# A tuned attention and two-layer kernel on one core: front reordered, W1 scaled between its loads, pair 1 in seven products, batch 1 mixed by VectorE

## The chip, the cores and the metric

One core of a Trainium2 chip runs the kernel. The metric is the time of one execution on the device in microseconds (us), given as the median of three runs. Engines: PE multiplies matrices (TensorE, with PEld its weight loads), DVE is VectorE, ACT is ScalarE, POOL is GpSimd, SP is SyncE. POOL and SP issue the transfers (DMAs); every one that converts from float32 to float16 goes through POOL's queue.

## What is computed

The inputs are q, k, v (4 batches, 8 heads, 768 tokens, 64 columns), 8 memory rows per head, a gain vector and two weight matrices W1 (512 x 2048) and W2 (2048 x 512).

```python
for c in range(24):                       # chunks of 32 queries
    keys = concat(mem_k, k[16 before .. 8 after the chunk])   # 8 + 56 rows
    a = softmax(q_c @ keys.T / 8)
    out[c] = a @ concat(mem_v, the same rows of v)
x = out, heads side by side               # (4, 768, 512)
xn = (x - mean) / sqrt(var + 1e-6) * g
y = x + relu(xn @ W1) @ W2
```

## The kernel before, in words

The tokens of a batch are 6 tiles of 128, in all 24 tiles t; two tiles make a pair u, 12 pairs. For each tile the chain is: `qk` (scores on PE, then `below_max` on DVE, a maximum at L325 and a subtraction at L326, then `weights`, the exponential on ACT at L332), `pt` (transpose of the weights on PE, L342, copy on ACT), `val` (`val_products` on PE at L356 into the two-bank tile `two`; `tokens` on DVE, L365 to L372, which divides by the sums and takes the mean; `shift`, which subtracts the mean, on ACT at L383 or POOL at L379), `turn_x` (transpose on PE at L408, DVE copy into xT at L414) and `root` (sum of squares on ACT, inverse square root on POOL). A pair then goes through `up` (8 steps of 8 products at L446 and a relu, L437 on ACT) and down to the output. `up_half` (L458) is `up` for one tile of pair 0.

The down product has two forms. `down` (L467) is the plain one: 8 steps of 4 products with 512 columns (L471), of which the last of each tile adds to the token and stores (L478). `down7` (L538) makes a pair's 2 x 2 blocks with seven products in place of eight: 7 steps of 8 products with 256 columns (L522), each followed by an addition on DVE (L529). It needs four sums of the relu's output (`r_sum`, L516) and four of W2 (`w2_sum`, L501), all on DVE.

Keys and values reach PE as transposes. For batch 0, `turn_k`, `turn_q` and `turn_v` (L214) transpose the raw data, and copies on DVE ("V") or ACT ("A") put it into the streams: `to_stream` (L227), `to_rows` (L234). V of batch 0 is turned back by `v_turn` (L284, copy L295). From batch 1 on, k and q are first interleaved by `mix` (L245, two copies of 96 x 1024 elements), then turned by `later_k` and `later_q` (L254); V is loaded in place by `load_v_head`.

Every engine takes its instructions in the order of the program, written out by hand: a front for pairs 0 and 1 (L597 to L805), and a plan (L807 to L892) that puts each function of pairs 2 to 11 on one of 16 steps of a pair; the even steps end with an `up`, the odd ones with a down step. `banks` and `use` say which PSUM banks the next functions take in turn. `warm` (L590) issues products of zeros that keep PE busy. POOL's loads share eight semaphores in turn, so that the ninth load waits for the first to land. `scale_w1` (L419) multiplies a quarter of W1 by the gain, four pieces a quarter, at L428 on POOL.

## Time and profile before

| what | us |
|---|---|
| median of three runs | 232.29 (232.07 to 232.44) |
| the profiled execution's own time | 232.79 |
| its span from first to last instruction | 231.1 |
| PE's first real stretch without large gaps begins (first `up`, L446) | 31.44 |
| PE's last product starts | 227.0 |

In the timeline a line gives start, duration, engine, source line, operation, the tile written and those read, the count, and in brackets the idle time ahead of it and what ended that. A product's duration includes its latency, so consecutive ones overlap; the spacing of their starts tells how fast PE runs. In the table of stretches, each engine has its busy time in that stretch.

| stretch, us | PE busy | DVE busy | ACT busy | POOL busy |
|---|---|---|---|---|
| 0 to 10 | 8.69 | 4.17 | 2.14 | 8.60 |
| 10 to 20 | 9.51 | 6.68 | 4.87 | 4.96 |
| 20 to 30 | 8.90 | 6.45 | 4.88 | 9.79 |
| 30 to 40 | 8.36 | 5.59 | 6.63 | 9.24 |
| 40 to 50 | 10.00 | 5.21 | 8.88 | 8.51 |
| 50 to 60 | 9.60 | 7.78 | 9.56 | 9.82 |
| 60 to 70 | 10.00 | 5.35 | 6.72 | 4.99 |
| 70 to 80 | 10.00 | 8.98 | 4.71 | 6.39 |
| 80 to 90 | 9.69 | 9.44 | 6.15 | 7.87 |

### The profile page before, as it was taken

Reading aid. Unit: us, or ns where it says so; the run is one execution under the profiler, and the core shown is the slowest. Engines: PE = TensorE matmul, PEld = TensorE weight load, DVE = VectorE, ACT = ScalarE, POOL = GpSimd, SP = SyncE. Lnnn points to the kernel's source line nnn. Section 1 sums busy time; section 2 is a strip of 40 time slices with the busy share of each in tenths; the row PEclk is TensorE's granted clock in tenths of the full one; section 3 lists DMA queues with packets and bytes.
Section 4 is the critical chain, followed back from the end, with each engine's and each line's share of the span. In section 5 each row is a group of like instructions: output and inputs, shape, how many; then the busy total and the mean of one; then the engine's idle time right before and its main releaser. Section 6 shows DMA issues by size and latency. Waiting matters only on the chain.

```text
span 231.1 us, 8487 instructions
## 1 busy us (share of the span) xinstructions
PE 221.9 (96%) x3693; PEld 189.3 (82%) x3693; DVE 156.4 (68%) x365; ACT 128.7 (56%) x241; POOL 114.7 (50%) x197
## 2 busy tenths in 40 slices
PE   7998888999999999999999999999999999999993
PEld 3575776875676889989989999999999999899982
DVE  3476755478288897797577796895684875646372
ACT  2244585999852739739646458468447265344310
POOL 7829998989935694912724945613031121220000
PEclk9999999999999999999999999999999999999999
DMA  5999999999995699873881992943102002011022
GB/s 76 191 206 205 213 215 196 143 114 70 84 179 114 90 120 112 131 99 41 139 119 29 137 156 55 110 89 70 48 0 94 3 3 91 3 45 48 0 94 94
DMA packets 43282, 23.25 MB, mean 101 GB/s; under 512 B 29884, under 2 KB 39676, under 8 KB 43172
## 3 DMA queue, kind: packets, MB, share of 16 engines
q0 software_dynamic: 38320, 14.48, 55.1%
q1 hardware_dynamic: 4924, 8.22, 12.8%
q8 instruction: 29, 0.48, 0.8%
q14 instruction: 9, 0.07, 0.1%
HBM read 29.02 MB, written 6.29 MB: 153 GB/s over the span
## 4 chain that ended last, share of the span: by engine, by line
PE 76%; DMA 6%; ACT 5%; DVE 4%; POOL 4%; issue 2%; POOLq 0%; DVEq 0%
PE upb L446 31%; PE dnb L522 25%; PE dnb L471 5%; DMA w1c<-in_moe_w_ch_dram 4%; PE one L254 3%; PE two L356 3%; PE one L315 3%; PE one L408 2%; DMA V<-in_v_dram 2%; ACT rT L437 2%; PE one L342 2%; POOL raw L111 2%; POOL w1c L428 1%; DVE KT L227 1%; ACT sq L394 1%
## 5 line engine op out<-in xcount | busy, mean ns | idle before, releaser
L446 PE MATMUL upb<-xT,w1c 128*128 128x256 f16 x736 | 94.8, 273 | 0.4 <-DVE xT L414 0.2
L446 PEld LDWEIGHTS <-w1c 128*128 128x128 f16 x736 | 77.9, 114 | 3.2 <-DVE xT L414 0.4
L437 ACT ACTIVATE rT<-upb 128x512 f16<-128x512 f32 x92 | 53.3, 594 | 34.9 <-PE upb L446 32.8
L529 DVE SCALAR_TENSOR_TENSOR xs<-dnb,rstd,xs 128x256 f32<-128x256 f32 x70 | 33.7, 481 | 27.2 <-PE dnb L522 26.7
L332 ACT ACTIVATE P<-sub 128x512 f16<-128x512 f32 x24 | 15.2, 634 | 37.9 <-DVE sub L326 37.9
L522 PEld LDWEIGHTS <-RS 128*128 128x128 f16 x320 | 30.9, 98 | 3.3 <-issue 0.2
L379 POOL TENSOR_SCALAR xn<-xs,nmean 128x512 f16<-128x512 f32 x18 | 13.6, 756 | 37.4 <-PE upb L446 20.6
L522 PE MATMUL dnb<-T,RS 128*128 128x256 f16 x240 | 30.8, 273 | 0.0
L398 POOL TENSOR_SCALAR veps<-ssq 128x1 f32<-128x1 f32 x24 | 4.8, 200 | 44.2 <-ACT sq L394 43.9
L522 PEld LDWEIGHTS <-rT 128*128 128x128 f16 x240 | 22.9, 98 | 2.3
L120 POOL DMA_DIRECT2D V<-in_v_dram x24 | 20.4, 852 | 0.7 <-PE dnb L522 0.7
L522 PE MATMUL dnb<-w2c,rT 128*128 128x256 f16 x160 | 20.6, 273 | 0.0
L516 DVE TENSOR_TENSOR RS<-rT 128x1024 f16<-128x1024 f16 (+2 forms) x21 | 13.9, 661 | 8.9 <-ACT rT L437 8.9
L325 DVE TENSOR_REDUCE nmx<-one 128x8 f32<-128x512 f32 x22 | 15.1, 685 | 4.7 <-PE one L315 4.7
L394 ACT ACTIVATE sq<-xs,nmean 128x512 f16<-128x512 f32 x24 | 17.3, 721 | 0.1
L366 DVE CUSTOM_DVE_ANT_1 xs<-two,rec 128x512 f32<-128x512 f32 x24 | 16.6, 691 | 0.8
L471 PE MATMUL dnb<-w2c,rT 128*128 128x512 f16 x64 | 16.3, 379 | 0.0
L125 POOL DMA_DIRECT2D V<-in_v_dram x24 | 15.9, 662 | 0.0
L326 DVE TENSOR_TENSOR sub<-one,nmx 128x512 f32<-128x512 f32 x22 | 15.2, 692 | 0.8
L347 ACT COPY PT<-one 128x512 f16<-128x512 f16 x21 | 12.2, 587 | 4.1 <-PE one L342 4.0
L402 POOL TENSOR_TENSOR rstd<-veps,mhalf 128x1 f32<-128x1 f32 x24 | 13.4, 560 | 2.0
L227 DVE COPY KT<-one 128x192 f16<-128x192 f16 (+1 forms) x22 | 11.2, 550 | 2.1 <-PE one L214 1.4
(112 smaller groups left out, 320.5 us busy)
## 6 DMA issues: line engine op xcount, KB each, us to landing
out_dram<-xs SPq DMA_DIRECT2D x23, 256.0 KB, 2.4
raw<-in_k_dram POOLq DMA_DIRECT2D x16, 192.0 KB, 5.3
raw<-in_q_dram POOLq DMA_DIRECT2D x12, 192.0 KB, 6.3
w1c<-in_moe_w_ch_dram POOLq DMA_DIRECT2D x4, 512.0 KB, 10.5
w2c<-in_moe_w_ch_dram POOLq DMA_DIRECT2D x4, 512.0 KB, 8.7
V<-in_v_dram POOLq DMA_DIRECT2D x24, 77.0 KB, 4.0
V<-V SPq DMA_DIRECT2D x3, 360.0 KB
V<-in_v_dram POOLq DMA_DIRECT2D x24, 44.0 KB, 3.7
```

The lines of the kernel that those rows point to most:

```text
L120: nc.gpsimd.dma_start(out=V[b % 2][72:128, 0 : NG - 1, h, 0:64], in_=dram(v, base + 16 * D, [[64, 56], [64 * 64, NG - 1], [1, 64]]),)
L125: nc.gpsimd.dma_start(out=V[b % 2][0:32, 1:NG, h, 0:64], in_=dram(v, base + 48 * D, [[64, 32], [64 * 64, NG - 1], [1, 64]]),)
L325: nc.vector.tensor_reduce(out=m, in_=scores, axis=AX.X, op=ALU.max)
L326: nc.vector.tensor_tensor(out=s.rearrange("p (c k) -> p c k", c=8), in0=scores, in1=free(m, 0, [[1, 8], [0, 64]]), op=ALU.subtract,)
L332: nc.scalar.activation(out=P[t % 3], in_=sub[t % 2], func=ACTF.Exp, scale=0.125)
L366: nc.vector.tensor_tensor_reduce(out=x.rearrange("p (h d) -> p h d", h=H), in0=free(two, 0, [[128, 8], [1, 64]]), in1=free(r, 0, [[1, 8], ...
L394: nc.scalar.activation(out=sq, in_=xs[t % 9], func=ACTF.Square, bias=nmean[t % 6], scale=1.0, accum_out=ssq[i],)
L437: nc.scalar.activation(out=o, in_=i, func=ACTF.Relu)
L446: nc.tensor.matmul(out=p[:, 256 * hb : 256 * hb + 256], lhsT=free(w1c[hc // 4][:, dt, :], hc % 4, [[4, 128]]), rhs=xT[u % 3][:, dt, :], st ...
L471: nc.tensor.matmul(out=p, lhsT=rT[u % 2][:, hc, 128 * i : 128 * i + 128], rhs=w2c[hc // 4][:, hc % 4, :], start=(hc == 0), stop=(hc == 15),)
L522: nc.tensor.matmul(out=p[:, 0:256], lhsT=left[:, n, :], rhs=right(n), start=(n == 0 and not add), stop=(n == 7), skip_group_check=add,)
L529: nc.vector.scalar_tensor_tensor(out=x, in0=p[:, 0:256], scalar=rstd[t % 9], in1=x, op0=ALU.mult, op1=ALU.add,)
```

## The change

- In the front, warm products go to the second half of `two` and there are 24 of them in place of 29; the banks are given out differently.
- The first q copies are split: each engine copies the columns of the first score tile, then those of the second.
- `below_max` of tile 1 is taken apart: its maximum comes after the last V^T copy, its subtraction after the first two `v_turn`, both of which DVE now copies, ahead of the first `pt`.
- POOL scales W1's first quarter ahead of the load of the third, and the second ahead of the load of the fourth.
- `mix` of batch 1 is done by DVE throughout and, for its first half, issued earlier, between the ups of pair 1.
- Pair 1's down product becomes `down7` with its sums; W2's last two sums move to steps 2 and 7 of pair 2; in pair 2 `root` moves by a step, the mix of batch 2's first half from step 14 to 10; the last `pt` of batch 1 moves from step 3 to 5 of pair 3.

```diff
-    def to_rows(b, pv, jj, engine, n, oct0):
+    def to_rows(b, pv, jj, engine, n, oct0, lo=0, hi=None):
+        hi = n if hi is None else hi
         copy_on(engine)(
-            out=free(QD[b % 2], 2 * jj * S + 8 * oct0, [[S, 2], [8, n], [1, 8]]),
-            in_=free(pv, 0, [[1, 2], [2, n], [2 * n, 8]]),
+            out=free(QD[b % 2], 2 * jj * S + 8 * (oct0 + lo), [[S, 2], [8, hi - lo], [1, 8]]),
+            in_=free(pv, 2 * lo, [[1, 2], [2, hi - lo], [2 * n, 8]]),
         )
...
-    def qk_products(t):
+    def qk_products(t, p=None):
-        p = slot()
+        p = slot() if p is None else p
...
+    def row_max(t, scores):
+        nc.vector.tensor_reduce(out=nmx[t % 2], in_=scores, axis=AX.X, op=ALU.max)
+    def less_max(t, scores):
+        nc.vector.tensor_tensor(
+            out=sub[t % 2].rearrange("p (c k) -> p c k", c=8), in0=scores,
+            in1=free(nmx[t % 2], 0, [[1, 8], [0, 64]]), op=ALU.subtract,
+        )
...
     load_octets(2, 1, v, 0, 48, 48)
-    load_w1(2)
-    load_w1(3)
...
-    banks["list"] = one + dnb + [upb[0]]
-    warm(7)
+    for c in range(2):
+        for dt in range(4):
+            scale_w1(c, dt, "P")
+        load_w1(2 + c)
+    idle = two[:, 512:1024]
+    warm(7, idle)
+    use(one[0], one[1], dnb[0], dnb[1])
...
-    warm(4)
+    warm(4, idle)
     for j in range(2):
         turn_k(0, 0, j, "VA"[j])
-    warm(1)
-    for j in range(2):
-        turn_q(0, 0, j, "VA"[j])
-    warm(2)
-    s0 = qk_products(0)
-    s1 = qk_products(1)
+    warm(1, idle)
+    q0 = [turn(raw[1][0], j, 32, one[j]) for j in range(2)]
+    for lo in (0, 16):
+        for j in range(2):
+            to_rows(0, q0[j], j, "VA"[j], 32, 0, lo, lo + 16)
+    s0 = qk_products(0, two[:, 0:512])
+    s1 = qk_products(1, dnb[0])
     below_max(0, s0)
+    use(upb[0], upb[1])
     turn_v(0, 0, "A")
     weights(0)
     turn_v(0, 1, "V")
-    warm(4)
+    row_max(1, s1)
+    warm(2, idle)
+    use(dnb[1], one[0], upb[0], upb[1])
+    v_turn(0, "V")
+    v_turn(1, "V")
+    less_max(1, s1)
+    use(one[1])
     pt(0)
-    v_turn(0, "A")
-    banks["turn"] += 1
-    v_turn(1, "V")
-    below_max(1, s1)
+    use(upb[0], upb[1])
     v2 = v_products(2)
     v3 = v_products(3)
     weights(1)
-    warm(1)
+    warm(1, idle)
     val_products(0)
     tokens(0)
     shift(0, "A")
-    warm(4)
+    warm(3, one[1])
+    use(dnb[1])
     pt(1)
-    for c in range(2):
-        for dt in range(4):
-            scale_w1(c, dt, "P")
     v_copy(2, v2, "V")
     v_copy(3, v3, "V")
-    warm(4)
-    banks["list"] = one
+    warm(4, one[1])
+    use(one[0])
     turn_x(0)
...
     up(1, 4)
+    mix(0, 0, "V")
     v_turn(11, "A")
...
     up(1, 6)
+    mix(1, 0, "V")
     root(3)
...
-    mix(0, 0, "V")
-    mix(1, 0, "A")
     down(0, 0)
...
-    mix(1, 1, "A")
+    mix(1, 1, "V")
...
-            at(u, 12, root, a)
+            at(u, 13, root, a)
...
-            at(3, 3, pt, c + 2)
+            at(3, 5, pt, c + 2)
...
-            at(w, 14 if w == 2 else 12, mix, 0, half, "V")
+            at(w, 10 if w == 2 else 12, mix, 0, half, "V")
...
-    at(2, 7, w2_sum, 2)
-    at(2, 9, w2_sum, 3)
-    for u in range(2, NP - 1):
+    at(2, 2, w2_sum, 2)
+    at(2, 7, w2_sum, 3)
+    for u in range(1, NP - 1):
         for m, step in ((0, 0), (1, 1), (2, 3), (3, 5)):
             plan.setdefault((u + 1, step), []).insert(0, (r_sum, (u, m)))
...
-            elif u == 2:
-                down(1, step // 2)
             elif step < 15:
                 down7(u - 1, step // 2)
```

More of the change, by code (lines that the diff above doesn't have):

```diff
@@ L321, in qk_products @@
         return p.rearrange("p (c k) -> p c k", c=8)
-    def below_max(t, scores):
-        m, s = nmx[t % 2], sub[t % 2]
-        nc.vector.tensor_reduce(out=m, in_=scores, axis=AX.X, op=ALU.max)
-        nc.vector.tensor_tensor(
-            out=s.rearrange("p (c k) -> p c k", c=8), in0=scores,
-            in1=free(m, 0, [[1, 8], [0, 64]]), op=ALU.subtract,
-        )
+    def row_max(t, scores):
[5 more added lines that the diff above has]
+        )
+    def below_max(t, scores):
+        row_max(t, scores)
+        less_max(t, scores)
     def weights(t):
```

## The prediction

> **What bounds the kernel now.** I read the page's first two parts, then stretches, then the timeline wherever TensorE (PE) waits.

> ```profile
> PE 221.9 (96%) x3693; PEld 189.3 (82%) x3693; DVE 156.4 (68%) x365; ACT 128.7 (56%) x241; POOL 114.7 (50%) x197
> ...
> PE   7998888999999999999999999999999999999993
> ```

> PE looks full throughout, but a busy PE need not be at its peak. The spacing of its starts tells more: 256-column products follow each other at 109 ns when nothing holds them. Summed over stretches, starts later than that spacing cost 4 to 5 us in each ten up to 40 us, and about 1 us in each ten after that, mostly the 0.1 us that each change of kind takes. So two things move the end: PE work removed after 40 us, and when the front (0 to 31 us, a chain of small steps) hands over to dense work.

> The front in the timeline (start, duration, engine, line, tile; idle time and releaser in brackets):

> ```profile
> 10.19 1.04 PE L593 MATMUL upb<-zeros 128*128 128x512 f16 x2
> 10.30 0.58 ACT L234 COPY QD<-one 128x512 f16<-128x512 f16 x1 [0.67 <-PE one L214]
> 11.15 1.04 PE L315 MATMUL dnb<-KT,QD 64*32 64x64 f16 x64
> ...
> 16.66 0.69 DVE L326 TENSOR_TENSOR sub<-dnb,nmx 128x512 f32<-128x512 f32 x1
> 17.27 0.20 DVE L365 RECIPROCAL rec<-two 128x8 f32<-128x8 f32 x1
> ...
> 18.08 5.36 POOL L428 TENSOR_SCALAR w1c<-w1c,g_col 128x512 f16<-128x512 f16 x8
> ...
> 18.43 0.72 ACT L383 ACTIVATE xn<-xs,nmean 128x512 f16<-128x512 f32 x1 [0.41 <-DVE nmean L372]
> ...
> 20.83 0.92 PE L458 MATMUL upb<-xT,w1c 128*128 128x128 f16 x13 [0.38 <-POOL w1c L428]
> 21.68 0.53 PE L214 MATMUL one<-identity,raw 96*64 96x96 f16 x16
> ```

> The scores wait for two warm products; the token normalisation waits for DVE's second subtraction; the first up products wait for POOL's W1 scaling. Later:

> ```profile
> 50.54 1.98 ACT L245 COPY raw<-raw 96x1024 f16<-96x1024 f16 x2
> 50.72 0.51 PE L254 MATMUL upb<-identity,raw 96*128 96x96 f16 x8 [0.23 <-DVE raw L245]
> ...
> 53.93 0.50 PE L254 MATMUL upb<-identity,raw 96*128 96x96 f16 x8 [0.18 <-ACT KT L227]
> ```

> ```profile
> 81.34 0.38 PE L342 MATMUL one<-identity,P 128*128 128x128 f16 x4 [0.31 <-DVE KT L227]
> ```

> These three starts come 0.41, 0.34 and 0.47 us after the normal spacing.

> **Part 1, the front.** I walk the chain with the durations above.

> Query copies. One of 512 columns takes 0.70 us on DVE and 0.58 on ACT; of 1024, 1.23 and 1.01. By that slope 256 columns take 0.43 and 0.37 (estimate; bounds zero and the whole 512-column row). ACT's first half starts at 10.30, ends 10.67; the two warm products are gone, so scores start at 10.7 for 11.15: 0.45 earlier.

> First half of the scores (0.64 us to its last result): the maximum starts at 11.4, subtraction ends 12.8, DVE's V^T copies run 13.2 to 14.2, the second maximum ends at 14.8, two V copies (0.42 each, overlapping) at 15.6, the second subtraction at 16.2. It ended at 17.35, so DVE's queue is 1.1 ahead. On PE the V turns now stand ahead of the transpose of the first weights: it moves from 14.54 to 14.6, ACT's copy to 15.6. The values then start at 15.7 for 16.26, and the reciprocal at 16.2 for 17.27, since the second subtraction no longer ends after them. ACT does the second exponential at 16.25 to 16.9, the shift at 17.3 for 18.43: **1.1 earlier**. Turn of x at 18.1, xT done at 19.0.

> W1. Landings (semaphores): first two quarters at 12.8 and 16.2. Eight scalings of 0.67 us (5.36/8) end their halves at 15.5 and 18.9, before xT. So the up products start at 19.0, run in one piece (0.9 us), and the k turn starts at 20.0 for 21.68. The second shift ends at 20.9 (22.05 before); its turn starts at 21.0 for 22.58, and the second half's q turn at 21.95 for 23.66 as it waits for DVE's copy. **Gain 1.7 us**, which the rest inherits.

> What W1 pushes back: loads of quarters 3 and 4 go out at 15.6 and 19.0 instead of 13.1 and 16.5. Ahead of them in the one POOL queue are transfers that land until 22.6, so it never runs empty, and landings stay at about 25.2 and 27.7. The w2 issues behind them come at about 20 and 23, earlier than 23.39 and 26.48. Quarters 3 and 4 are scaled by 27.9 and 30.6 (33.0 before); their users need them at 29.7 and 33.4. If that cover were gone, each us of a late landing past 29.7 would cost one. Batch 1's k and q still land at 38.7 to 50.7 in queue order, and are first used at about 42 and 46, with the pairs behind at about 51 and 55.

> Two gaps called "issue" stay: 0.66 at 26.79 and 0.94 at 38.59. They lie 512 PE instructions apart and the page counts 29 instruction packets of 0.48 MB: PE waits for its own code. The instruction stream keeps its length within some ten, so I cost them at nothing; bounds from both gone (-1.6) to half again as long (+0.8).

> **Part 2, batch 1's interleave.** DVE's mixes (0.75 a pair) go to 44.2 and 48.1, where DVE idles 2.18 us (before 46.38) and 1.18 us (before 49.31). ACT loses 1.98 us at 50.54 and 2.00 at 58.83. The k turn at 50.72 then waits for nothing (0.41). The token chain, DVE idle, starts at 50.5 for 50.92, the shift ends at 52.2 for 53.14, the first k copy at 53.0 for 53.88, while PE would reach the q turn at 53.2: the 0.34 goes too. **0.75 us.** If the mixes met a busy DVE instead, they'd cost up to 0.75 each; raw data landed long before.

> **Part 3, pair 1 by seven products.** Eight quarter products (0.86 to 0.87 us) become seven of 0.87: PE loses **0.8 us**. DVE gains four sums (0.68 each) and seven additions (0.48) for two of 0.75: +4.6 us. In the stage from 59.6 to 77.7 the stretches show DVE 12.4 of 18.1 us busy. The added work fills that: sums and the first w2 difference fit into the 3.8 us in which DVE waits for scores (before 64.43), but the first maximum comes some 0.3 us late, so the second exponential delays the relu behind it by about 0.25 and the fifth up product with it. By my queue of DVE (each at its spacing) it catches up by the end of pair 2; PE arrives at pair 3 some 0.8 to 1.0 earlier. There the weights' transpose at step 5 no longer meets the k copy (0.47 gone), but the second k turn then waits about 0.55 for the subtraction that frees its bank. Net **0.6 to 0.7**. Bounds: 1.3 (both stalls free) and, if half of the 5.7 us idle can't be used, -1.0.

> **Sum.** 1.7 + 0.75 + 0.65 = 3.1 us. Against the profiled execution's 232.79 that gives 229.7; the three plain runs have a median of 232.29, 0.5 lower, so I forecast **229.2 us** for them.

> **A rule on the clock.** Warm products follow each other at 0.43 us until 13.55 and at 0.216 from about 14.0 on, though the granted clock reads 1.00 in every stretch. Five of 29 go. [...] The trace agrees with half rate up to 13.55; what decides it no row shows.

> **Rivals.**
> - *The forecast*, all three parts: 228.4 to 230.0. Chance 0.62.
> - *DVE binds pairs 2 and 3.* Part 3 then returns nothing or loses up to 1.0, parts 1 and 2 stay: 229.8 to 230.9. For: no idle DVE from 60.6 to about 76 in my queue, and 15.0 of 18.0 us busy in the next stage. Against: the idle lies ahead of the point where it is needed. Chance 0.15.
> - *The front gives back its gain*: the doubling a look later, or the two code waits growing by what is saved between them (they end 2.3 us after their packets start): parts 2 and 3 plus 0.5, 230.4 to 231.4. Chance 0.11.
> - *Slower: the clock stays halved until the dense work.* Place: 14 to 31 us. PE's starts there need about 5.8 us per ten at full rate, so 9.9 us; twice that, with the 7.1 us of gaps absorbing only about half, costs 5 to 6 us against a gain of 3.1: 234 to 235. It decides once half rate lasts past about 24 us (5.8 us of added issue, half of it on the path). For: warm products removed. Against: ten to fourteen us of the same transposes remain. Chance 0.08.
> - *No effect*: the landings, not the chain, set the front. Against: every landing precedes its use by over 1 us. 232.3. Chance 0.04.

> **Range.** 228.2 to 231.0: the forecast's span, DVE's rival, and part of the third. A measurement of this kernel can tell about 0.2% from no change, 0.46 us: faster 0.88, same 0.04, slower 0.08.

> **What would show it.** Right: scores' products at 10.7, shift at 17.3, first up products in one piece near 19.0, k turn near 20.0, dense up products at 29.7 for 31.44; no stall at the first batch-1 turn; no four-quarter products after pair 0; 0.6 us or more between the shift of the starts at 58 us and at 90. Wrong: 0.43 us warm spacing after 14; an up product waiting for w1c; PE waits on DVE longer than 0.3 us between 58 and 85; code waits that grow.

## The result and the profile after

The changed kernel takes 233.63 us (median of six runs, 233.03 to 234.04) beside 232.39 for the kernel before (six runs, 232.07 to 232.70): ratio 1.005, 95% interval 1.0033 to 1.0067. It is **slower by 0.5%**, where 229.2 was forecast and 231.0 was the upper end of the range. The profiled execution took 233.83, its span is 232.1.

Lines of the changed kernel (numbers shifted by the new functions): up L452, relu L443, seven-product down L528 with additions L535 and sums L522, maximum L325, subtraction L328, exponential L338, weights' transpose L348, values L362, tokens L371 to L378, shift L389 (ACT) or L385 (POOL), x transpose L414, mix L246, batch 1's and later turns L255, k turn L214, scaling of W1 L434, warm products L599.

The page of after, its first two parts (busy time of each engine, then 40 slices of 5.8 us):

```profile
PE 218.9 (94%) x3712; PEld 190.6 (82%) x3712; DVE 162.8 (70%) x380; ACT 124.6 (54%) x237; POOL 115.6 (50%) x197
...
PE   7699987999998799999999999999999999999993
```

PE's busy time fell by 3.0 us, but the span grew by 1.0, so PE now waits 4 us more. Behind the first 41 us one place in the row of digits shows it, the 87 at slices 13 and 14 (70 to 81 us), where the page of before had 99. The table of stretches says the same. First after, then before (stretch, then busy time and count of PE, PEld, DVE, ACT, POOL, the granted clock, DMA):

```profile
70.00:80.00 10.00, 7.81 (x164) 6.69 (x162) 6.74 (x17) 3.50 (x8) 4.00 (x8) 1.00 0.65 122
```

```profile
70.00:80.00 10.00, 10.00 (x173) 7.47 (x172) 8.98 (x21) 4.71 (x11) 6.39 (x10) 1.00 0.53 90
```

All engines are less busy than before in that stretch, so none of them is the bound; something that is not an engine holds them. The timeline of after there, one line from each link:

```profile
65.33 1.17 POOL L111 DMA_DIRECT2D raw<-in_k_dram  x2
...
70.62 0.42 PE L362 MATMUL two<-V,PT 64*32 64x65 f16 x32
...
73.22 0.76 DVE L246 COPY raw<-raw 96x1024 f16<-96x1024 f16 x2 [2.80 <-DMA raw<-in_k_dram]
73.90 0.20 DVE L371 RECIPROCAL rec<-two 128x8 f32<-128x8 f32 x1
75.19 0.69 POOL L385 TENSOR_SCALAR xn<-xs,nmean 128x512 f16<-128x512 f32 x1 [3.25 <-DVE nmean L378]
...
75.94 0.40 PE L414 MATMUL one<-identity,xn 128*128 128x128 f16 x4 [1.48 <-POOL xn L385]
...
77.10 0.63 ACT L338 ACTIVATE P<-sub 128x512 f16<-128x512 f32 x1 [5.78 <-DVE sub L328]
...
78.27 1.03 PE L452 MATMUL upb<-xT,w1c 128*128 128x256 f16 x8 [0.71 <-ACT rT L443]
```

Read it downward. The load of batch 2's k goes out at 65.33 and lands at 72.2 and 73.1 (its two halves, in one queue with V's loads). DVE reaches the mix at 70.4 and **stands 2.80 us**. Behind it in DVE's queue is the reciprocal of tile 7, whose values left PE at 71.0 and were ready; it runs at 73.90. The shift, the x transpose and the scores follow, and PE loses 1.48 and then 0.71 us (ACT idles 5.78 us for the late exponential, and the relu that the up product needs stands behind it). In the kernel before, the same load lands at 72.8 and its mix stands at step 14:

```profile
64.16 1.16 POOL L111 DMA_DIRECT2D raw<-in_k_dram  x2
...
76.03 0.75 DVE L245 COPY raw<-raw 96x1024 f16<-96x1024 f16 x2
```

No idle time stands ahead of this copy. Moving it from 76 to about 70 took it from behind the landing to ahead of it.

Start of the same PE work in both profiled executions, after less before (a minus is earlier): scores of tile 0 -1.9 us; values of tile 0 +0.2; k turn -0.62; first dense up -0.90; pair 1's first up (behind the code wait at 38 us) -0.48; pair 2's first up -1.06; its seventh -0.98; **its eighth +0.69**; pair 3's first +0.59; the end +1.06. So three things are to be explained: the 1.7 forecast at 20 us became 0.5 at 40; one mix cost 1.7 at once; and the seven products saved less than said. (Most of the scores' 1.9 is not the front's work: after ran at full rate from 4.24 us on, before from 13.81, where its scores started at 11.15; the same old front started them at 9.62 in a run at full rate from 4.56 on.)

### The profile page after: what moved, and what is told of

Same layout as the page of the kernel before. It is cut to its first block, busy times and chain, and to the rows that moved or that the text cites. A ratio compares the mean times of both kernels' runs of the same rounds, so it can differ in the third digit from the quotient of the medians.

```text
span 232.1 us, 8538 instructions
## 1 busy us (share of the span) xinstructions
PE 218.9 (94%) x3712; PEld 190.6 (82%) x3712; DVE 162.8 (70%) x380; ACT 124.6 (54%) x237; POOL 115.6 (50%) x197
## 4 chain that ended last, share of the span: by engine, by line
PE 81%; DMA 6%; DVE 4%; POOL 3%; issue 2%; ACT 2%; POOLq 0%; DVEq 0%
PE upb L452 32%; PE dnb L528 26%; PE two L362 3%; DMA raw<-in_k_dram 3%; PE one L255 3%; PE dnb L477 3%; PE one L414 3%; DMA raw<-in_v_dram 2%; PE one L316 2%; PE one L348 2%; POOL raw L111 2%; ACT rT L443 1%; DVE xs L372 1%; PE one L599 1%; DVE KT L227 1%
## 5 line engine op out<-in xcount | busy, mean ns | idle before, releaser
L452 PE MATMUL upb<-xT,w1c 128*128 128x256 f16 x736 | 94.7, 273 | 1.0 <-ACT rT L443 0.7
L452 PEld LDWEIGHTS <-w1c 128*128 128x128 f16 x736 | 77.9, 114 | 2.8 <-DVE xT L420 0.8
L443 ACT ACTIVATE rT<-upb 128x512 f16<-128x512 f32 x92 | 53.6, 595 | 36.6 <-PE upb L452 34.8
L535 DVE SCALAR_TENSOR_TENSOR xs<-dnb,rstd,xs 128x256 f32<-128x256 f32 x77 | 36.9, 479 | 27.0 <-PE dnb L528 26.6
L528 PEld LDWEIGHTS <-RS 128*128 128x128 f16 x352 | 33.8, 98 | 3.7 <-issue 0.2
L338 ACT ACTIVATE P<-sub 128x512 f16<-128x512 f32 x24 | 15.2, 634 | 39.1 <-DVE sub L328 39.1
L528 PE MATMUL dnb<-T,RS 128*128 128x256 f16 x264 | 33.9, 273 | 0.0
L385 POOL TENSOR_SCALAR xn<-xs,nmean 128x512 f16<-128x512 f32 x18 | 12.8, 710 | 38.3 <-PE upb L452 20.5
L528 PEld LDWEIGHTS <-rT 128*128 128x128 f16 x264 | 25.1, 98 | 2.5
L528 PE MATMUL dnb<-w2c,rT 128*128 128x256 f16 x176 | 22.7, 273 | 0.0
L522 DVE TENSOR_TENSOR RS<-rT 128x1024 f16<-128x1024 f16 (+2 forms) x23 | 15.2, 662 | 9.2 <-ACT rT L443 9.2
L120 POOL DMA_DIRECT2D V<-in_v_dram x24 | 20.9, 871 | 1.0 <-PE dnb L528 0.7
L400 ACT ACTIVATE sq<-xs,nmean 128x512 f16<-128x512 f32 x24 | 17.3, 721 | 0.1
L372 DVE CUSTOM_DVE_ANT_1 xs<-two,rec 128x512 f32<-128x512 f32 x24 | 16.6, 691 | 0.8
L408 POOL TENSOR_TENSOR rstd<-veps,mhalf 128x1 f32<-128x1 f32 x24 | 15.0, 625 | 2.0
L328 DVE TENSOR_TENSOR sub<-one,nmx 128x512 f32<-128x512 f32 x22 | 15.2, 691 | 0.8
L325 DVE TENSOR_REDUCE nmx<-one 128x8 f32<-128x512 f32 x22 | 15.0, 683 | 0.8 <-PE one L316 0.8
L125 POOL DMA_DIRECT2D V<-in_v_dram x24 | 15.5, 647 | 0.0
L420 DVE COPY xT<-one 128x512 f16<-128x512 f16 x21 | 8.8, 418 | 4.7 <-PE one L414 4.6
L255 PEld LDWEIGHTS <-raw 96*128 96x128 f16 x192 | 10.6, 97 | 1.7 <-issue 0.5
```

The source lines that it names most:

```text
L120: nc.gpsimd.dma_start(out=V[b % 2][72:128, 0 : NG - 1, h, 0:64], in_=dram(v, base + 16 * D, [[64, 56], [64 * 64, NG - 1], [1, 64]]),)
L125: nc.gpsimd.dma_start(out=V[b % 2][0:32, 1:NG, h, 0:64], in_=dram(v, base + 48 * D, [[64, 32], [64 * 64, NG - 1], [1, 64]]),)
L255: nc.tensor.matmul(out=pv[:, 96 * r : 96 * r + 96], lhsT=mixed[i][0:96, jj, r, :], rhs=identity[0:96, 0:96], is_transpose=True, start=True ...
L328: nc.vector.tensor_tensor(out=sub[t % 2].rearrange("p (c k) -> p c k", c=8), in0=scores, in1=free(nmx[t % 2], 0, [[1, 8], [0, 64]]), op=AL ...
L338: nc.scalar.activation(out=P[t % 3], in_=sub[t % 2], func=ACTF.Exp, scale=0.125)
L372: nc.vector.tensor_tensor_reduce(out=x.rearrange("p (h d) -> p h d", h=H), in0=free(two, 0, [[128, 8], [1, 64]]), in1=free(r, 0, [[1, 8], ...
```

## The experiments

Two theories after the first reading. **Q**: DVE's queue stands behind the landing of batch 2's k (2.8 us at 70 to 73), and all else is a gain of about 1.5. **S**: DVE is simply too full in pairs 2 and 3. For the front, **C**: PE's own code arrives at set times while the load queue is full. In the trace's packet records the instruction queue moves 16,384 bytes at a time. In the records of PE (weight loads, products and its few semaphore instructions counted together) the longest waits called "issue" stand at records 450, 962 and 1474 in every kernel in which they occur, 512 apart, each ending 2.2 to 2.5 us after a packet's start. Packets come some 6 us apart up to 36 us (before: 12.12, 18.21, 24.52, 30.33, 36.32; after: 11.96, 18.08, 23.62, 29.92, 36.03). Against it **K**, the author's guess: what PE's clock does in the front sets its time, and warm products keep the clock up.

**Where the lost time is: the mix at step 14 again.**

```diff
-            at(w, 10 if w == 2 else 12, mix, 0, half, "V")
+            at(w, 14 if w == 2 else 12, mix, 0, half, "V")
```

> The changed kernel with the mix of batch 2's first half back at step 14 of pair 2. Theory Q (DVE's queue stands 2.8 us behind a mix that waits for its load, and everything after it in the queue is late): DVE goes on to the second value tile's normalisation at once, the x turn that came 1.64 us late and the up product 0.9 us late are no longer late, and pair 3 begins about 0.8 us earlier than in the kernel before instead of 0.6 later: 231.7 to 232.4 us, 1.3 to 1.9 below the changed kernel's 233.6. Theory S (DVE has too much to do in pair 2 with the seven-product sums, wherever the mix stands): DVE stays behind, 233.2 to 233.8.

Measured: 231.50 us (230.85 to 233.62; ratio to before 0.997, 0.9944 to 0.9996), a little under Q's range. One number undoes 2.1 us and turns slower into slightly faster. DVE still has all of its added work, so S falls.

**The load earlier, the mix left at step 10.**

```diff
-            at(w, 5 if w == 2 else 1, load_octets, 0, half, k, b, 48 * half, 48)
+            at(w, 0 if w == 2 else 1, load_octets, 0, half, k, b, 48 * half, 48)
```

> The changed kernel with the mix left at step 10, but the k load that it waits for issued at step 0 of pair 2, ahead of that step's V loads, instead of step 5. Theory Q: the load lands some 3 us earlier (70 us instead of 73.1), the wait of 2.8 us falls to under 0.5, and the time is that of the kernel with the mix at step 14, within 0.4: 231.7 to 232.6. Theory S: no change, 233.2 to 233.8.

Measured: 232.06 us (231.08 to 233.25; 0.9977, 0.9956 to 0.9997). The load's second half lands at 72.0, later than expected, so the mix still waits 0.84 us (2.80 before this edit), more than the 0.5 that Q allowed:

```profile
71.99 0.76 DVE L246 COPY raw<-raw 96x1024 f16<-96x1024 f16 x2 [0.84 <-DMA raw<-in_k_dram]
```

The lead over before stays at 0.26 and 0.25 us from pair 2's seventh up to its eighth, where after lost 1.7. Both cures work: it is the order of mix and landing.

**The parts alone.** The front with everything else as before (and step 14), then the seven products with everything else as before (and step 14).

```diff
     up(1, 4)
-    mix(0, 0, "V")
...
     up(1, 6)
-    mix(1, 0, "V")
...
+    mix(0, 0, "V")
+    mix(1, 0, "A")
     down(0, 0)
...
-    at(2, 2, w2_sum, 2)
-    at(2, 7, w2_sum, 3)
-    for u in range(1, NP - 1):
+    at(2, 7, w2_sum, 2)
+    at(2, 9, w2_sum, 3)
+    for u in range(2, NP - 1):
```

> The kernel before with the front part of the change alone (banks, split copies, V turns, W1 scaling between its loads); pair 1 is plain, the mixes are as before. The prediction's theory (front gives 1.7): 230.5 to 230.9. Theory C (the front is held by the arrival of PE's code, records 450, 962 and 1474, some 6 us per 256 records while the load queue is full): PE's record 1474 is reached 0.2 to 0.6 earlier than before's 38.6 whatever the front's chain does, and the time is 231.7 to 232.2. Theory N (the front gives nothing): 232.2 to 232.6.

Measured: 233.37 us (232.41 to 234.29; 1.0026, 1.0006 to 1.0047): **slower**, and above every theory's number. Its profile has the first code packet at 13.59, and PE waits 2.33 us for it at 15.84.

```diff
-    at(2, 7, w2_sum, 2)
-    at(2, 9, w2_sum, 3)
-    for u in range(2, NP - 1):
+    at(2, 2, w2_sum, 2)
+    at(2, 7, w2_sum, 3)
+    for u in range(1, NP - 1):
```

> The kernel before with the seven-product part alone: down7 for pair 1, its sums, W2's last sums at steps 2 and 7, root at step 13, the last weights' transpose at step 5; mix stays at step 14. Theory Q: PE saves a product of 0.87 us and the stall of 0.47, and pays about 0.55 at the second k turn of pair 3: 231.4 to 232.0. Theory S: DVE is late by what the sums add, 232.4 to 233.5.

Measured: 232.19 us (231.92 to 233.04; 0.9979, 0.996 to 0.9998), less gain than Q said. Its lead grows from 0.25 to 1.78 us between pair 2's seventh up and pair 3's third, 0.22 of it only because the moved transpose now runs behind that up. Pair 3's second k turn then starts 0.8 us late: at 84.19, where the down step ahead of it starts at 82.51 and takes 0.87. A gain of 0.5 is left. The same line in the kernel with the mix at step 14 (first experiment; down step at 81.68, so again 0.8 late), and below it in the kernel before:

```profile
83.35 0.50 PE L255 MATMUL one<-identity,raw 96*128 96x96 f16 x8 [0.64 <-DVE sub L328]
```

```profile
84.93 0.51 PE L254 MATMUL one<-identity,raw 96*128 96x96 f16 x8
```

The turn needs the bank whose scores DVE is still subtracting. The last weights' transpose of batch 1, moved to step 5, gives the bank order in which this wait arises.

**That transpose at step 4** (on the first experiment's kernel).

```diff
-            at(3, 5, pt, c + 2)
+            at(3, 4, pt, c + 2)
```

> The changed kernel with the mix at step 14 (231.5 measured) and the last weights' transpose of batch 1 at step 4 of pair 3, ahead of that step's scores, instead of step 5. If the 1.0 us by which pair 3's second k turn starts late comes from the score bank that it shares (freed by DVE's subtraction), the turn then follows the transpose's bank and starts at once: 230.4 to 230.9. If DVE is simply late there, the wait moves to the next start that needs DVE: 231.2 to 231.7.

Measured: 230.99 us (229.92 to 232.84; 0.9937, 0.9905 to 0.9969), 0.5 below the first experiment and between the two ranges expected. The intervals of the two kernels overlap, but the profiles say the same: behind pair 2's seventh up the lead grows by 1.1 us here and by 0.5 there. The second k turn then waits for nothing, and a smaller wait comes later:

```profile
82.88 0.51 PE L255 MATMUL one<-identity,raw 96*128 96x96 f16 x8
...
86.03 0.40 PE L414 MATMUL one<-identity,xn 128*128 128x128 f16 x4 [0.27 <-POOL xn L385]
```

**The front: more code, less code, later loads.** All three start from the first experiment's kernel.

```diff
-    warm(7, idle)
+    for _ in range(20):
+        nc.tensor.matmul(
+            out=idle[:, 0:16], lhsT=zeros[:, 0:128], rhs=zeros[:, 0:16], start=True, stop=True,
+        )
+    warm(6, idle)
```

> The changed kernel with the mix at step 14, and one of the first seven warm products replaced by twenty products of 16 zero columns, issued in the first 4 us: 38 PE records more, about the same PE time. Theory C (the front is held by the arrival of PE's code, about 256 records in 6 us): every later piece of the program comes up to 38/256 x 6 = 0.9 us later; PE waits at the same record numbers 450, 962, 1474, at about the same times: 232.0 to 232.5. Theory K (only the clock's phase matters): 231.2 to 231.8, as without them.

Measured: 234.85 us (234.27 to 235.9; 1.0096, 1.0059 to 1.0134), 3.3 above the first experiment and far more than C's number. Two causes mix here: the waits at records 450 and 1474 are 2.63 and 2.00 us, and the granted clock is half from 12.88 to 19.71 and again from 40.19 to 43.6 us in the trace's clock records. The run doesn't separate them. The wait keeps its record number although other work stands there: with 38 records more ahead, record 450 is a product of L214 and no longer of L348.

```profile
14.56 0.29 PE L214 MATMUL upb<-identity,raw 96*64 96x96 f16 x1 [2.63 <-issue]
...
40.05 0.22 PE L316 MATMUL one<-KT,QD 64*32 64x64 f16 x5 [2.00 <-issue]
```

```diff
-    warm(2, idle)
...
-    warm(1, idle)
     val_products(0)
...
-    warm(3, one[1])
...
-    warm(4, one[1])
...
-    warm(2, one[1])
```

> The changed kernel with the mix at step 14 and without the twelve warm products behind the scores: 24 PE records fewer, 2.6 us of warm products less. Theory C: 24/256 x 6 = 0.5 us earlier at record 1474's place: 230.8 to 231.2. Theory K: the clock is granted later or withdrawn more often, 232 to 234.

Measured: 231.12 us (230.04 to 232.22; 0.9939, 0.9914 to 0.9963). Twelve warm products fewer cost nothing, although the clock became full only at 24.04 in its profile: the rival "clock halved until dense" (234 to 235) doesn't come from these.

```diff
-    for c in range(2):
-        load_w2(c)
...
-    for c in range(2, 4):
-        load_w2(c)
...
     load_octets(1, 1, q, 1, 48, 48)
+    for c in range(4):
+        load_w2(c)
```

> The changed kernel with the mix at step 14 and W2's four loads issued behind batch 1's k and q loads (near 39 us) instead of at 21 to 25 us, so that the load queue runs empty near 28 to 31 and 36 to 38 us. Theory C: the code packets near 30 and 36 us start sooner after their block is entered, PE's wait at record 1474 falls from 0.85 to under 0.4 and it is passed at 37.4 to 37.8 instead of 38.2: 230.7 to 231.2. If the code's arrival has nothing to do with the load queue: 231.3 to 231.8, or later where W2 comes late.

Measured: 237.79 us (236.34 to 239.14; 1.0213, 1.0168 to 1.0258): W2 lands at 50.0 to 57.0, and pair 0's down product waits for it. The total says nothing of C, but the first 40 us do: from 27.9 to 30.8 us no load was under way, the packets came at 27.22 and 32.09 in place of about 30 and 36, record 1474 passed at 36.82 with no wait, and the up product behind it started at 37.97, 1.36 earlier than in the first experiment.

**What each part is worth, with the waits found so far removed.** Less code together with step 4; step 4 with the old front in place of the new; the interleave alone (only the batch-1 mixes of the change's diff); the front alone with less code.

> The changed kernel with batch 2's first mix back at step 14, the last weights' transpose of batch 1 at step 4 of pair 3, and the 12 warm products behind the first scores left out (24 fewer PE records ahead of the dense work). Theory A (code arrival and stalls add up): the two edits gained about 0.5 us (transpose at step 4) and 0.4 us (fewer warm products) against the same kernel without them (231.5), at different places, so together 230.4 to 230.8 us. Theory B (the front's time is set by the clock's phase, not by what PE is fed): fewer warm products are worth nothing, 230.9 to 231.3.

> The kernel before with all of the change but its front: seven products for pair 1, the interleave of batch 1 by VectorE, batch 2's first mix left at step 14, the last weights' transpose of batch 1 at step 4 of pair 3. Theory A (the front's gain is held up by the code's arrival and is worth about nothing): as the same kernel with the new front, 230.8 to 231.2 us. Theory F (the front is worth the 0.6 us by which the k turn came earlier in the profile): 231.5 to 231.9. Theory G (the front costs 0.9 us, as the run of the front alone had it): 230.0 to 230.3.

> The kernel before with batch 1's interleave alone done by VectorE between the ups of pair 1. Prediction's term: 0.75 us, 231.7 us. From the profile after (the lead grew by 0.58 us between the start of batch 1's turns and pair 2's start): 231.8 to 231.9. A rival in which pair 2's scores hold the lead back: 232.3 to 232.5.

> The front part alone, with the 12 warm products behind the first scores left out (24 fewer PE records). Theory A (code arrival holds the front): 0.4 to 0.9 us below the front alone (233.4): 232.5 to 233.0. Theory B (the clock's phase sets it, warm products help): 233.4 to 235.

Measured, in that order: 230.81 (229.96 to 231.53; 0.9917, 0.9885 to 0.995); 230.71 (230.46 to 231.21; 0.9918, 0.9889 to 0.9946); 231.71 (231.54 to 232.69; 0.9966, 0.9947 to 0.9984); 233.08 (231.51 to 234.53; 1.0009, 0.998 to 1.0039). The kernel **without** the front is as fast as any with it. The interleave alone is worth 0.8 us, its forecast. Seven products with step 4 are worth the 1.0 us between the second and third of these. Less code took 0.2 to 0.4 us off three kernels with the new front, each within its interval.

Why the old front is as good shows where it ran at full rate from 4.56 us on (the interleave alone):

```profile
12.60 0.40 PE L342 MATMUL one<-identity,P 128*128 128x128 f16 x4 [0.17 <-ACT P L332]
12.93 0.41 PE L284 MATMUL dnb<-identity,KT 128*64 128x128 f16 x8
14.47 0.41 PE L284 MATMUL upb<-identity,KT 128*64 128x128 f16 x8 [1.13 <-issue]
...
26.75 0.32 PE L315 MATMUL one<-KT,QD 64*32 64x64 f16 x17 [0.66 <-issue]
```

The first weights' transpose started 1.94 us ahead of the kernel before, and the first dense up product 0.04 ahead. The first code wait left about 0.6 of the lead (second weights' transpose 17.47, before 18.07), the up product that waits for W1's scaling 0.23 (20.60, before 20.83), and the second code wait 0.04. And the new front, where it ran at full rate (the run with the load at step 0):

```profile
14.84 0.40 PE L348 MATMUL one<-identity,P 128*128 128x128 f16 x4 [1.18 <-issue]
...
17.72 0.72 ACT L389 ACTIVATE xn<-xs,nmean 128x512 f16<-128x512 f32 x1 [1.33 <-DVE nmean L378]
...
19.41 1.05 PE L464 MATMUL upb<-xT,w1c 128*128 128x128 f16 x16
...
20.39 0.88 PE L214 MATMUL one<-identity,raw 96*64 96x96 f16 x16
...
26.91 0.27 PE L316 MATMUL one<-KT,QD 64*32 64x64 f16 x12 [1.50 <-issue]
```

Its k turn is 1.29 us ahead of the kernel before (21.68). At 26.91 it waits for its code until the lead is gone: before passed the same record at 26.79, after a wait of 0.47, and the first dense up product starts at 31.52 here, 31.44 there. The line of before:

```profile
26.79 0.32 PE L315 MATMUL one<-KT,QD 64*32 64x64 f16 x17 [0.47 <-issue]
```

**Room in the load queue, with either front.** Both leave out the loads and scalings of W1's third and fourth quarters and load W2 behind the first half of batch 1, so they do less work than the kernel before. The edit with the new front:

```diff
+    w1c[2], w1c[3] = w1c[0], w1c[1]
...
-        load_w1(2 + c)
...
-    for c in range(2):
-        load_w2(c)
...
-    for c in range(2, 4):
-        load_w2(c)
...
-    for c in range(2, 4):
-        for dt in range(4):
-            scale_w1(c, dt, "P")
...
+    for c in range(4):
+        load_w2(c)
     load_octets(0, 1, k, 1, 48, 48)
```

> The kernel with the old front, seven products, interleave and the weights' transpose at step 4, with room in the load queue: the third and fourth quarters of W1 are neither loaded nor scaled (the first two stand in for them, so the output is not the reference's), and W2 is loaded behind the first half of batch 1. Theory A (the code's arrival behind the loads sets PE's time at records 962 and 1474): both waits shrink to under 0.2 us, first dense up products at 30.5 to 31.0, total 229.5 to 230.3 us, if W2 lands before 50. Theory B (clock or chain sets the front): waits change, the time stays within 0.3 of 230.7.

> The same with the new front (the same work left out: W1's third and fourth quarters neither loaded nor scaled, the output not the reference's). Theory A: with the code in time the new front's lead shows, 0.6 to 1.0 us below the old front with room, so 228.6 to 229.6 us. Theory B: the new front isn't ahead by itself, or the clock takes the lead back: within 0.3 us of the old front with room, or above it.

Measured: 230.13 us with the old front (229.13 to 231.26; 0.9892, 0.9861 to 0.9924), 229.89 with the new (228.94 to 232.05; 0.9895, 0.9858 to 0.9933). The packets come at about 22 and 27.5 us in place of 24.5 and 30, the wait at record 962 goes in both, and the first dense up product comes a whole us earlier than in before: 30.38 and 30.39. The wait at record 1474 shrinks only to 0.34 in the old. The two still end together, against A: the room comes after the packet at 18 us, and the new front is held already at record 450 (by 1.35 us at 14.56), then runs at half rate from 15.23 to 18.65. So the code's arrival is shown to hold the time at 27 us. The work that these two leave out isn't seen to matter there (between 21 and 45 us the profile of before has no wait of PE for W1), but the totals contain it too, and are not the price of the code waits alone. Whether the new front would lead with the first packet in time wasn't tried.

## Why the prediction was wrong, point by point

**The step that failed most** is in none of its terms: the move of batch 2's first mix from step 14 to 10. The prediction called part 2 "batch 1's interleave", put the mixes on DVE's idle time, remarked that "raw data landed long before", and never looked at the batch-2 load that this mix waits for. Its landing, 72.8 us, stood in the trace of before, and the move went to about 70. Cost: 233.63 less 231.50, **2.1 us**; with the mix put back, slower becomes faster.

**Part 1, the front, 1.7 us: worth nothing.** The chain was walked rightly where the clock was full: shift forecast 17.3, seen 17.72; first up products in one piece, forecast near 19.0, seen 19.41; k turn 20.0, seen 20.39. In the changed kernel's own profile, where the granted clock was half from 11.06 to 17.89 us, these came at 18.29, 20.07 and 21.05. The failed step is "I cost them at nothing" for the two code waits: they don't shift with the work, they end when the code arrives. The prediction had their bound on that side at +0.8 and the case as a rival ("the two code waits growing by what is saved between them", 0.11). And it took the wait at record 450 for absent, because before passed it at 15.05 without waiting: its packet had started at 12.12, and 2.2 to 2.5 us later the code was there. With the front left out, 230.71, with it 230.99 (intervals overlap); alone it costs 0.9 (ratio 1.0006 to 1.0047), with less code 0.6 (0.998 to 1.0039, which holds no difference). That small loss isn't explained. The clock may be part of it: the mean granted clock was under 0.995 in 5 of the 12 runs of the front alone (median 233.61, the other seven 232.68) and in 6 of 93 runs of the kernel before. With less code it was so in 8 of 12, at no difference (233.13 and 233.08), so it isn't shown to be.

**Part 2, the interleave, 0.75 us: mechanism right, the number partly by luck.** Both stalls went, and the cover (DVE idle at 44 and 48 us) held. But in the profile the lead grows by 0.29 and 0.28 us at the two turns, in place of 0.41 and 0.34, so they give 0.57. The 0.8 measured alone (0.4 to 1.2 by the interval of its ratio) agrees with either.

**Part 3, seven products, 0.65 us net: mechanism right, one term too small.** The 0.8 of PE and the 0.47 of the stall came (1.3 in sum; the lead grew by 1.5 in pairs 2 and 3, with 0.22 of moved work). The new wait of the second k turn, put at 0.55, took 0.8. Net 0.5 by the profile and 0.3 by the times alone, and 1.0 with the transpose at step 4, near the 1.3 that was given for both stalls free. The rival "DVE binds pairs 2 and 3" didn't come: with the mix at step 14 DVE does all of the added work, and that kernel is faster than before.

**Clock.** The prediction weighed a doubling that came a look later; no run shows what such a look is, and that part of the rival's 230.4 to 231.4 is the author's estimate. What the runs showed in its place: in the trace's clock records the granted rate is full from 13.81 on in before (no record stands ahead of it; warm products start 0.43 us apart until 13.55 and 0.216 from 13.89); in after it is full from 4.24, half from 11.06, full from 17.89. In other kernels with the same front the steps lie at 9.02 alone; at 4.67, 11.49 and 18.32; at 8.72, 15.54 and 18.96. The distances are 6.8 and 3.4 us, and the start differs from run to run. Half rate came back at 11.06 although PE's longest wait between 5 and 11 us was 0.69 us; from 6.74 us on much of its work was transposes. What brings half rate back isn't shown, nor that five warm products fewer did: the kernel with twelve fewer still was no slower. In its rival of a clock that stays halved, the prediction's own terms give 6.3 us (9.9 less half of 7.1), not 5 to 6; nothing else hangs on it.

**Sum.** Mix at step 10 +2.1, front +0.3 (0.9 alone), interleave -0.8, seven products with step 5 about -0.4: +1.2, as measured (233.63 less 232.39). The front's 0.3 is not clear of noise. The best kernel found that computes the whole is the one without the front, 230.71, 0.8% below before; it and the one with less code can't be told apart.

## What to carry to other kernels

An instruction that waits for a transfer is moved with its landing time in hand, not with the idle time of its engine: in this kernel all that stands behind it in its engine's program waits too, and the price appears two engines further (here DVE's mix waits 2.80 us, POOL's shift comes late with it, and PE stands 1.48 us for the shift). A front that "issue" waits follow need not get shorter when its chain does: look at which record the waits stand, and if it is the same one at the same time whatever comes ahead, what has to move is the code's arrival (here an emptier load queue moved it; that fewer instructions help wasn't clear of noise). And a change with three parts is tried as three: one moved step undid what two of them won.
